# Two score banks masked apart, the first chunk's loads halved over two queues, fewer warm-up products, and a new order of the work

## The chip, the core and the metric

The kernel runs on one core of a Trainium2 chip. The metric is device time in microseconds (us) of one execution; an execution under the profiler also leaves a trace. The core has a matrix engine (TensorE: PE, with its weight loads as PEld), a vector engine (VectorE: DVE), a scalar engine (ScalarE: ACT), a general engine (GpSimd: POOL) and SyncE (SP), which issues most of the transfers. Each works through its own list of instructions in order; semaphores hold an instruction until what it needs is there.

## What is computed

Two batches of 768 positions, model width 512 (8 heads of 64). Three layers follow each other:

```python
# 1 retention: a decayed running state per head
state = gamma * state + k_t (outer) v_t ;  x_t = scale * q_t @ state
# 2 spectral layer
theta = x @ w_theta ;  zr, zi = x * cos(theta), x * sin(theta)
u = x + w_tok_r @ zr + w_tok_i @ zi          # over the 768 positions
x = u + relu(u @ w_ch)
# 3 gated layer
h = gelu(x @ w_in) ;  u, v = halves of h
v = (v - mean) / sqrt(var + 1e-6) * g_ln ;  v = w_sg @ v + b_sg
out = x + (u * v) @ w_out
```

## The kernel before

**Tiling.** Retention runs over 12 chunks of 128 positions (`i` = 0 to 11, six per batch). A chunk has, on PE, `scores` (8 products of 64x128 by 128x128, both operands float32), `outer` (8 products for the new state) and `attend` (8 products with the masked scores, and for all but a batch's first chunk 8 more with the state); on DVE, `mask` (the two score banks times a causal triangle, line 470), the state's `grow` (lines 512 and 519) and the copy of `x` out of PSUM (line 570); on ACT, `fade_v_heads` (line 488: eight small scalings of V); on POOL, `shrink` (line 522). The trace shows each float32 product of these as two records.

**The large products** are done three times over on split values: every operand is a high part in float32r (ACT, line 302) and a low remainder (DVE, line 308), and `terms3` multiplies high by high, low by high and high by low. They are 128x512 products: `angle` (six of them per half), `mix_main` (six), `mix_rest` (twelve of half width), then layers of twelve. A `turn` is four transposes on PE (line 664). The weights of these arrive packed and take two DVE operations at line 394 before they can be split.

**PSUM** has eight banks, which the kernel holds in one tile, `banks`; a planner gives every intermediate result a bank. The mask of a chunk reads both of its score banks with one operation, as a slice from the lower bank `a` to the higher bank `b` in steps of `b - a`:

```python
in0=banks.rearrange("p (b n t) -> p b n t", b=8, n=NP)[:, a : b + 1 : b - a]
```

**Loads.** `load_qk` and `load_kv` bring a chunk's Q and K, and its K and V, 512 KB each. They go through SP's queue, but for the first chunk's `kv`, which ACT issues (line 433). `dec` (the decay factors, line 453) is SP's second transfer, and the fade of every chunk reads it.

**Order.** `ORDER` is a table of operation numbers. `Plan.schedule` walks it with assumed durations, gives buffers and banks, and the operations are then issued by their assumed start. The order on an engine is thus set by that table. Ahead of everything PE does eight products on a zeroed tile; `keep_warm` puts products of the identity with itself in places where the planner expects PE to wait early on (before `WARM`, 34):

```python
gap = o.start - done
if done < WARM and gap > 0.25:
    keep_warm(idle[0], int(gap / 0.24))
```

Of the kernel before, what the change touches and what calls it, by code (L numbers as in the profile page):

```python
# [14 lines left out]
ALU = mybir.AluOpType  # L15
# [3 lines left out]
P = 128  # L19
NCH = S // P  # L20
# [42 lines left out]
class Plan:  # L63
# [3 lines left out]
    BEGIN = {"PE": 4.2, "ACT": 2.3, "DVE": 1.4, "POOL": 2.0, "SP": 0.8, "SPA": 0.8}  # L67
    FLY = 8

# [3 lines left out]
    def op(self, eng, dur, fn, r=(), w=(), prio=0.0, port=False, after=(), until=None, lev=None):  # L73
# [13 lines left out]
        o.lev = prio if lev is None else lev  # L87
        for x in r:
            self.res[x][1].append(o)
# [6 lines left out]

    def schedule(self, order):

# [6 lines left out]
        port = sent = skew = 0.0  # L105
        landed, last = [], {}
        for o in (self.ops[k] for k in order):
            t = max([engines[o.eng], *(d.end + (self.LAT if d.eng != o.eng else 0.0) for d in o.deps)])
# [4 lines left out]
            for b in o.bufs:  # L113
                if b.base is None:
                    room = free[b.of]
                    b.base = min(range(len(room)), key=lambda k: room[k])
                    if room[b.base]:
                        t = max(t, room[b.base] + self.LAT)
                    room[b.base] = math.inf
            o.start = t  # L120
            if o.eng in ("SP", "SPA"):
                engines[o.eng] = t + 0.45
                if sent < t + 1.0:
                    sent, skew = t + 1.4, 0.3
                sent += o.dur
                skew = min(2.8, skew + 0.25 * o.dur)
                o.end = sent + skew
                if o.eng == "SP":
                    landed.append(o.end)
            else:  # L130
                engines[o.eng] = o.end = t + o.dur
# [65 lines left out]
def retention_spectral_gmlp(  # L197
# [248 lines left out]
    def retention(i):  # L446
# [117 lines left out]
        if c > 0:  # L564
            r += [qk, ("state", c % 2)]
# [652 lines left out]
```

## Time and profile before

| | |
|---|---|
| median of 3 runs | 383.7 us (383.68 to 383.85) |
| profiled execution, its own time | 384.12 us |
| its span, first to last instruction | 382.4 us |
| PE busy | 374.5 us, 98% |
| DVE busy | 269.9 us, 71% |
| ACT busy | 173.6 us, 45% |
| chain that ended last | PE 97%, DMA 1%, DVE 1% |

The span is what the rows below measure; the execution's own time holds some 1.7 us more around it. Busy counts every record, identity products of `keep_warm` too, so a busy PE is not all useful work. Idle time of an engine that nobody waits for costs nothing.

### The profile page before, as it was taken

What the parts mean: (1) busy time and instruction counts of PE and PEld (TensorE: products, weight loads), DVE (VectorE), ACT (ScalarE), POOL (GpSimd) and SP (SyncE); (2) the same over time, 40 slices, a digit from 0 to 9 for tenths busy, and PEclk for the clock granted to TensorE, in tenths of its full rate; (3) what the DMA queues carried; (4) which work ended last, traced back from release to release, by engine and by line L of the source; (5) the groups of instructions that cost most, each with busy time, mean ns of one, the idle gap of its engine ahead of it and who ended that gap; (6) DMA issues with size and microseconds to landing.
All of it is one profiled execution on the core that took longest, in us unless ns stands there. A gap on an engine that the chain in (4) does not pass through costs nothing.

```text
span 382.4 us, 5777 instructions
## 1 busy us (share of the span) xinstructions
PE 374.5 (98%) x2404; PEld 317.2 (83%) x2404; DVE 269.9 (71%) x396; ACT 173.6 (45%) x292; POOL 15.1 (4%) x18
## 2 busy tenths in 40 slices
PE   8999999998999989999999999999999999999996
PEld 7878888886899868888899888888888888898885
DVE  1689899796887678586647548895996774628522
ACT  4577987633246524446322434755364662202000
POOL 1021040001200001000000000000000000000000
PEclk9999999999999999999999999999999999999999
DMA  8999018115326301630423001000000000000206
GB/s 311 413 409 416 23 33 315 68 41 219 111 111 257 129 0 35 241 132 36 153 96 110 2 27 27 2 28 0 3 0 0 3 0 0 2 0 2 82 2 248
DMA packets 10203, 39.06 MB, mean 102 GB/s; under 512 B 1216, under 2 KB 2240, under 8 KB 7744
## 3 DMA queue, kind: packets, MB, share of 16 engines
q1 hardware_dynamic: 10032, 38.15, 26.4%
q10 hardware_dynamic: 144, 0.52, 0.3%
q8 instruction: 19, 0.31, 0.3%
q14 instruction: 8, 0.07, 0.1%
HBM read 35.53 MB, written 3.15 MB: 101 GB/s over the span
## 4 chain that ended last, share of the span: by engine, by line
PE 97%; DMA 1%; DVE 1%; issue 0%
PE banks L282 95%; PE banks L664 2%; DMA b<-qkv 1%; DVE b L470 1%; DVE b L672 0%; DVE xb L570 0%; DVE b L1043 0%
## 5 line engine op out<-in xcount | busy, mean ns | idle before, releaser
L282 PE MATMUL banks<-b,b 128*128 128x512 f32 (+2 forms) x1788 | 332.9, 352 | 2.7 <-DVE b L470 2.7
L282 PEld LDWEIGHTS banks<-b,b 128*128 128x128 f32 (+1 forms) x1788 | 277.6, 183 | 50.7 <-issue 4.2
L302 ACT ACTIVATE b<-b 128x512 fp32r<-128x512 f32 (+1 forms) x61 | 50.6, 847 | 84.1 <-DVE b L394 31.6
L308 DVE TENSOR_TENSOR b<-b,b 128x512 fp32r<-128x512 f32 (+1 forms) x61 | 56.3, 939 | 12.5 <-ACT b L302 11.1
L394 DVE SCALAR_TENSOR_TENSOR b<-b 128x1024 int32<-128x1024 int32 x32 | 39.2, 1224 | 2.4 <-ACT b L374 1.9
L805 ACT ACTIVATE b<-banks 128x512 f32<-128x512 f32 x24 | 13.8, 590 | 31.0 <-PE banks L282 29.6
L470 DVE TENSOR_TENSOR b<-banks,causal 128x1024 f32<-128x1024 f32 x12 | 14.7, 1222 | 15.4 <-PE banks L282 15.3
L813 DVE SCALAR_TENSOR_TENSOR b<-b,banks 128x512 f32<-128x512 f32 x24 | 16.1, 684 | 13.4 <-ACT b L805 13.4
L302 ACT ACTIVATE b<-xa 128x512 fp32r<-128x512 f32 (+1 forms) x26 | 16.9, 666 | 18.8 <-DVE xa L793 7.8
L282 PEld LDWEIGHTS banks<-b 64*128 64x128 f32 (+1 forms) x352 | 17.9, 170 | 5.3 <-issue 2.7
L282 PE MATMUL banks<-b 64*128 64x128 f32 (+1 forms) x352 | 21.2, 264 | 0.5 <-DMA b<-qkv 0.5
L374 ACT ACTIVATE b<-b 128x1024 f32<-128x1024 f32 x16 | 18.1, 1138 | 5.3 <-DMA b<-wts 5.3
L823 ACT ACTIVATE b<-b 128x512 f32<-128x512 f32 x24 | 14.7, 627 | 10.6 <-DVE b L813 10.6
L308 DVE TENSOR_TENSOR b<-xa,b 128x512 fp32r<-128x512 f32 (+1 forms) x26 | 19.2, 742 | 0.4 <-ACT b L302 0.2
L829 DVE SCALAR_TENSOR_TENSOR b<-b,banks 128x512 f32<-128x512 f32 x24 | 16.2, 682 | 4.2 <-ACT b L823 2.4
L984 DVE SCALAR_TENSOR_TENSOR b<-banks,gcol,brow 128x512 f32<-128x512 f32 x12 | 8.7, 748 | 14.0 <-PE banks L282 14.0
L488 ACT ACTIVATE b<-b,dec 128x64 f32<-128x64 f32 x64 | 16.0, 337 | 3.9 <-DMA dec<-decays 3.9
L522 POOL TENSOR_TENSOR state<-grown,dec 128x256 f32<-128x256 f32 x8 | 11.7, 1458 | 113.8 <-DVE grown L519 96.9
L672 DVE TENSOR_TENSOR b<-banks,b 128x1024 f32<-128x1024 f32 x12 | 14.6, 1218 | 1.2 <-ACT b L647 1.1
L914 ACT ACTIVATE b<-b,rstd 128x512 f32<-128x512 f32 x12 | 9.3, 805 | 6.9 <-DVE rstd L903 6.9
L302 ACT ACTIVATE b<-xb 128x512 fp32r<-128x512 f32 (+1 forms) x13 | 8.6, 668 | 7.6 <-DVE xb L793 3.5
L383 DVE TENSOR_SCALAR b<-b 128x1024 int32<-128x1024 int32 x16 | 11.4, 713 | 0.8 <-DMA b<-wts 0.8
(58 smaller groups left out, 180.5 us busy)
## 6 DMA issues: line engine op xcount, KB each, us to landing
b<-wts SPq DMA_DIRECT2D x16, 1024.0 KB, 4.8
b<-qkv SPq DMA_DIRECT2D x23, 512.0 KB, 9.6
out<-b SPq DMA_DIRECT2D x11, 256.0 KB, 2.7
b<-wsg SPq DMA_DIRECT2D x9, 256.0 KB, 5.1
xa<-wts SPq DMA_DIRECT2D x2, 1024.0 KB, 10.8
xb<-wts SPq DMA_DIRECT2D x1, 1024.0 KB, 8.6
b<-qkv ACTq DMA_DIRECT2D x1, 512.0 KB, 4.9
brow<-bvec SPq DMA_DIRECT2D x1, 384.0 KB, 5.3
```

Source lines behind the costliest of these rows:

```text
L282: nc.tensor.matmul(out=o, lhsT=l, rhs=r, start=start, stop=stop)
L302: act(words, lambda: A.activation(out=hi(), in_=src(), func=AF.Copy), prio=prio, r=r, **k)
L308: lambda: E.tensor_tensor(out=lo(), in0=src(), in1=hi().bitcast(F32), op=ALU.subtract),
L374: lambda: A.activation(out=words(1).bitcast(F32), in_=words(1).bitcast(F32), func=AF.Copy, scale=REBIAS),
L394: lambda scalar=scalar, op=op: V.scalar_tensor_tensor(out=words(0), in0=words(1), scalar=scalar, in1=words(0), op0=op, op1=ALU.bitwise_or,),
L470: V.tensor_tensor(out=ap(at[i]).rearrange("p (h n t) -> p h n t", h=2, n=NP), in0=banks.rearrange("p (b n t) -> p b n t", b=8, n=NP)[:, a ...
L488: A.activation(out=v, in_=v, func=AF.Copy, scale=dk[:, h : h + 1])
L672: V.tensor_tensor(out=z2, in0=ap(tp)[:, None, :].to_broadcast([P, 2, 512]), in1=z2, op=ALU.mult)
L805: lambda: A.activation(out=ap(s), in_=ap(t), func=AF.Square),
L813: lambda: V.scalar_tensor_tensor(out=ap(s), in0=ap(s), scalar=1.0 / GA, in1=ap(t), op0=ALU.add, op1=ALU.mult),
L823: lambda: A.activation(out=ap(s), in_=ap(s), func=AF.Tanh, scale=GA * GC),
L829: lambda: V.scalar_tensor_tensor(out=ap(o), in0=ap(s), scalar=1.0, in1=ap(t), op0=ALU.add, op1=ALU.mult),
```

## The change

Four things change. `mask` becomes two operations of half the size, one for each score bank, and each names only its own bank. The first chunk's two loads become four: the upper 64 rows of each go by SP's queue, the lower 64 by ACT's. `keep_warm` acts only on expected waits over 0.8, and for 0.5 less of each. And the planner gets other assumed durations, separate lags between engines and costs for a change of product form, and `ORDER` is a new table, so that nearly all operations stand in another order; after the change there are four identity products in one place, where there were twenty in three.

```diff
@@ -64,13 +64,14 @@
 
 
     LAT = 0.15
-    BEGIN = {"PE": 4.2, "ACT": 2.3, "DVE": 1.4, "POOL": 2.0, "SP": 0.8, "SPA": 0.8}
+    BEGIN = {"PE": 4.9, "ACT": 2.3, "DVE": 1.4, "POOL": 2.0, "SP": 0.8, "SPA": 0.8}
     FLY = 8
+    OVER = {"ACT": 0.097, "DVE": 0.083, "POOL": 0.03}
 
     def __init__(self, room):
         self.ops, self.res, self.room = [], {}, room
 
-    def op(self, eng, dur, fn, r=(), w=(), prio=0.0, port=False, after=(), until=None, lev=None):
+    def op(self, eng, dur, fn, r=(), w=(), prio=0.0, port=False, after=(), until=None, lev=None, form="main"):
         deps, bufs = set(after), []
         for x in r:
             deps.update(self.res.setdefault(x, ([], []))[0])
...
+    def lag(self, a, b):
+        if a == "PE":
+            return 0.2 if b != "PE" else 0.0
+        if b == "PE":
+            return 0.1
+        return 0.06 if a in ("SP", "SPA") else 0.035 if b != "POOL" else 0.08
+
+    def switch(self, a, b):
+        tiled = ("scores", "outer", "attend")
+        if a in ("main", "turn") and b in tiled:
+            return 0.09 if a == "main" else 0.23
+        return {"attend": 0.09 * (b != "outer"), "outer": 0.07}.get(a, 0.0) * (a != b)
+
...
 ORDER = [
-    56, 57, 58, 84, 83, 0, 111, 110, 59, 60, 61, 87, 62, 64, 63, 85, 65, 137, 138, 66, 7, 75, 86,
...
+    56, 57, 58, 59, 60, 86, 87, 0, 115, 114, 61, 62, 64, 63, 88, 67, 91, 90, 65, 142, 68, 143, 89,
...
 ]
 
 
...
@@ -414,30 +436,22 @@
 
     load = {}
 
-    def load_qk(i):
+    def load_half(i, k):
         b, c = divmod(i, NCH)
-        load[i, 0] = Buf("pair")
-        dma(
-            512,
-            lambda: nc.sync.dma_start(out=ap(load[i, 0]), in_=qkv[b, c, 0]),
-            w=[load[i, 0]],
-            prio=early(i) - 12,
-            after=[gate[i - 3]] if i >= 3 else (),
-        )
-
-    def load_kv(i):
-        b, c = divmod(i, NCH)
-        load[i, 1] = Buf("pair")
-        dma(
-            512,
-            lambda: (nc.scalar if i == 0 else nc.sync).dma_start(
-                out=ap(load[i, 1]), in_=qkv[b, c, 1]
-            ),
-            eng="SPA" if i == 0 else "SP",
-            w=[load[i, 1]],
-            prio=early(i) - 11,
-            after=[gate[i - 3]] if i >= 3 else (),
-        )
+        x = load[i, k] = Buf("pair")
+
+        def rows(queue, a, e):
+            queue.dma_start(out=ap(x)[a:e], in_=qkv[b, c, k][a:e])
+
+        t = dict(prio=early(i) - 12 + k, after=[gate[i - 3]] if i >= 3 else ())
+        if i == 0:
+            dma(256, lambda: rows(nc.sync, 0, 64), w=[(x, "top")], **t)
+            dma(256, lambda: rows(nc.scalar, 64, P), eng="SPA", w=[(x, "low")], **t)
+        else:
+            dma(512, lambda: rows(nc.sync, 0, P), w=[(x, "top"), (x, "low")], **t)
+
+    def landed(x):
+        return [(x, "top"), (x, "low")]
 
     gate = {}
     xhl, at = {}, {}
@@ -446,8 +460,8 @@
     def retention(i):
         b, c = divmod(i, NCH)
         t = early(i)
-        load_qk(i)
-        load_kv(i)
+        load_half(i, 0)
+        load_half(i, 1)
         qk, kv = load[i, 0], load[i, 1]
         if i == 0:
             dma(264, lambda: nc.sync.dma_start(out=dec, in_=decays), w=["dk"], prio=t - 10.9)
@@ -455,26 +469,26 @@
 
         def scores():
             q, k = ap(qk)[:, 0:512], ap(qk)[:, 512:1024]
-            s = sorted(sc, key=lambda x: x.base)
             for p in range(NP):
                 for h in range(2):
                     rows = slice(h * D, (h + 1) * D)
                     cols = slice(p * P, (p + 1) * P)
-                    mm(ap(s[h])[:, cols], k[rows, cols], q[rows, cols], True, True)
-
-        pe(1.08, scores, r=[qk], w=sc, prio=t)
+                    mm(ap(sc[h])[:, cols], k[rows, cols], q[rows, cols], True, True)
+
+        pe(1.09, scores, form="scores", r=landed(qk), w=sc, prio=t)
         at[i] = Buf("pair")
 
-        def mask():
-            a, b = sorted(x.base for x in sc)
-            V.tensor_tensor(
-                out=ap(at[i]).rearrange("p (h n t) -> p h n t", h=2, n=NP),
-                in0=banks.rearrange("p (b n t) -> p b n t", b=8, n=NP)[:, a : b + 1 : b - a],
-                in1=causal[:, None, None, :].to_broadcast([P, 2, NP, P]),
-                op=ALU.mult,
-            )
-
-        dve(1024, mask, ps=True, r=sc, w=[at[i]], prio=t + 1)
+        for h in range(2):
+
+            def mask(h=h):
+                V.tensor_tensor(
+                    out=ap(at[i])[:, h * 512 : (h + 1) * 512].rearrange("p (n t) -> p n t", n=NP),
+                    in0=ap(sc[h]).rearrange("p (n t) -> p n t", n=NP),
+                    in1=causal[:, None, :].to_broadcast([P, NP, P]),
+                    op=ALU.mult,
+                )
+
+            dve(512, mask, ps=True, r=[sc[h]], w=[(at[i], h)], prio=t + 1)
 
         def fade_v():
             v3 = ap(kv)[:, 512:1024].rearrange("p (h d) -> p h d", h=H)
...
@@ -560,10 +574,10 @@
                         c == 0 or p == NP - 1,
                     )
 
-        r = [kv, (kv, 1), at[i]]
+        r = [*landed(kv), (kv, 1), (at[i], 0), (at[i], 1)]
         if c > 0:
-            r += [qk, ("state", c % 2)]
-        gate[i] = pe(0.98 if c == 0 else 2.0, attend, r=r, w=[xp], prio=t + 3)
+            r += [*landed(qk), ("state", c % 2)]
+        gate[i] = pe(0.93 if c == 0 else 1.95, attend, form="attend", r=r, w=[xp], prio=t + 3)
         keys = [("x", b, c, d) for d in range(NP)]
         dve(
             512,
...
@@ -1129,9 +1143,9 @@
     for o in plan.schedule(ORDER):
         if o.eng == "PE":
             gap = o.start - done
-            if done < WARM and gap > 0.25:
+            if done < WARM and gap > 0.8:
                 idle = [k for k in range(8) if used.get(k, 0.0) <= done and k not in [b.base for b in o.bufs]]
-                keep_warm(idle[0], int(gap / 0.24))
+                keep_warm(idle[0], int((gap - 0.5) / 0.24))
             done = o.end
         if o.eng == "ACT" and not loaded:
             nc.scalar.preload_act_table_set("silu_and_others")
```

PE's first rows before, from the eight products on the zeroed tile; `b_96` is chunk 0's qk (so `banks<-b_96` is its scores), `b_98` its kv, `b_118` its masked scores, `ident` the identity; `b_101` and `b_103` are chunk 1's kv and qk:

```order
L282 MATMUL banks<-state_82 128x128 x8
L282 MATMUL banks<-b_96 128x128 x8
L282 MATMUL banks<-ident 128x128 x14
L282 MATMUL banks<-b_98 64x64 x8
L282 MATMUL banks<-b_118,b_98 64x128 x8
L282 MATMUL banks<-b_103 128x128 x8
L664 MATMUL banks<-ident,xa_85 128x128 x4
L282 MATMUL banks<-b_101 64x64 x8
L282 MATMUL banks<-ident 128x128 x2
L282 MATMUL banks<-b_103,state_83 64x128 x8
L282 MATMUL banks<-b_188,b_101 64x128 x8
L282 MATMUL banks<-ident 128x128 x4
```

The same place after the change; `b_99` is now chunk 0's kv and `b_120` its masked scores, `b_103` and `b_105` are chunk 1's qk and kv:

```order
L304 MATMUL banks<-state_82 128x128 x8
L304 MATMUL banks<-b_96 128x128 x8
L304 MATMUL banks<-ident 128x128 x4
L304 MATMUL banks<-b_103 128x128 x8
L304 MATMUL banks<-b_120,b_99 64x128 x8
L304 MATMUL banks<-b_99 64x64 x8
L678 MATMUL banks<-ident,xa_85 128x128 x4
L304 MATMUL banks<-b_105 64x64 x8
L304 MATMUL banks<-b_103,state_83 64x128 x8
L304 MATMUL banks<-b_160,b_105 64x128 x8
```

Four identity products are left of fourteen, the two and the four further down are gone, and chunk 1's scores and chunk 0's attend now stand ahead of chunk 0's outer.

PE before, in batch 1, around the attend of chunk 10 (its two rows read `state_82` and `b_1235`); the 128x512 rows are parts of `mix_main`, the last row is chunk 10's outer:

```order
L282 MATMUL banks<-b_619,b_1239 128x512
L282 MATMUL banks<-b_640,b_1227 128x512
L282 MATMUL banks<-b_720,state_82 64x128 x8
L282 MATMUL banks<-b_1235,b_1175 64x128 x8
L282 MATMUL banks<-b_619,b_1227 128x512
L282 MATMUL banks<-b_619,b_1239 128x512
L282 MATMUL banks<-b_640,b_1227 128x512
L282 MATMUL banks<-b_619,b_1227 128x512
L282 MATMUL banks<-b_619,b_1239 128x512
L282 MATMUL banks<-b_640,b_1227 128x512
L664 MATMUL banks<-ident,xb 128x128 x4
L282 MATMUL banks<-b_1175 64x64 x8
```

PE after the change, where the same chunk's small products stand; `64x64` rows are outers of chunks 10 and 9, `128x128` rows the scores of chunks 9, 11 and 10, `64x128` rows the attends of chunks 9, 10 and 11, and the last row a turn:

```order
L304 MATMUL banks<-b_846 64x64 x8
L304 MATMUL banks<-b_728 64x64 x8
L304 MATMUL banks<-b_1155 128x128 x8
L304 MATMUL banks<-b_1152 128x128 x8
L304 MATMUL banks<-b_1170 128x128 x8
L304 MATMUL banks<-b_1155,state_83 64x128 x8
L304 MATMUL banks<-b_1254,b_728 64x128 x8
L304 MATMUL banks<-b_1170,state_82 64x128 x8
L304 MATMUL banks<-b_1285,b_846 64x128 x8
L304 MATMUL banks<-b_1152,state_83 64x128 x8
L304 MATMUL banks<-b_1267,b_837 64x128 x8
L678 MATMUL banks<-ident,xb 128x128 x4
```

The last three chunks' small products, which stood in separate places among the large ones, now follow each other in one run.

SP before and after, the first rows (`dec` is the decay factors, `xb<-wts` the first packed weight):

```order
L422 DMA b_96<-qkv 128x1024
L453 DMA dec<-decays 128x524
L433 DMA b_101<-qkv 128x1024
L422 DMA b_103<-qkv 128x1024
L363 DMA xb<-wts 128x2048
L433 DMA b_106<-qkv 128x1024
L422 DMA b_108<-qkv 128x1024
```

```order
L444 DMA b_96<-qkv 64x1024
L444 DMA b_99<-qkv 64x1024
L467 DMA dec<-decays 128x524
L444 DMA b_103<-qkv 128x1024
L444 DMA b_105<-qkv 128x1024
L385 DMA xb<-wts 128x2048
L444 DMA b_108<-qkv 128x1024
L444 DMA b_110<-qkv 128x1024
```

Chunk 0's kv has come to SP's queue as a half, and chunk 1's qk now stands ahead of its kv.

## Rows read from the trace of the kernel before

**Rows 1.** The page's first line: the span of the profiled execution.

```profile
span 382.4 us, 5777 instructions
```

**Rows 2.** Waits of PE: engine, line waited for, us in total, times, longest.

```profile
PE banks L282 <- DVE b L470: 2.7, 2, 1.4
PE banks L282 <- DMA b<-qkv: 0.5, 1, 0.5
```

**Rows 3.** Timeline of PE, start: start, us, operation, records, idle time before.

```profile
1.26 3.78 PE L282 MATMUL banks<-state 128*128 128x128 f32 x16 [1.26 <-DVE state L261]
5.51 1.91 PE L282 MATMUL banks<-b 64*128 64x128 f32 x16 [0.47 <-DMA b<-qkv]
7.35 3.39 PE L282 MATMUL banks<-ident 128*128 128x128 f32 x28
10.67 0.69 PE L282 MATMUL banks<-b 128*64 128x64 f32 x16
...
14.45 0.71 PE L282 MATMUL banks<-ident 128*128 128x128 f32 x4
...
17.14 1.16 PE L282 MATMUL banks<-ident 128*128 128x128 f32 x8
...
24.27 1.66 PE L282 MATMUL banks<-b,b 128*128 128x512 f32 x6
```

**Rows 4.** Timeline of ACT and DVE, start.

```profile
6.43 3.93 ACT L488 ACTIVATE b<-b,dec 128x64 f32<-128x64 f32 x16 [3.94 <-DMA dec<-decays]
...
7.54 1.23 DVE L470 TENSOR_TENSOR b<-banks,causal 128x1024 f32<-128x1024 f32 x1 [6.33 <-PE banks L282]
...
12.28 0.69 DVE L570 TENSOR_TENSOR xa<-banks,dec 128x512 f32<-128x512 f32 x1 [0.42 <-PE banks L282]
```

**Rows 5.** Two stretches of the start: engines busy, granted PE clock, DMA share, GB/s.

```profile
1.20:3.70 2.50, 2.44 (x11) 2.44 (x12) 0.01 (x1) 1.28 (x1) 0.59 (x3) 1.00 0.68 208
1.20:5.00 3.80, 3.73 (x16) 3.49 (x16) 0.01 (x1) 1.28 (x1) 0.59 (x3) 1.00 0.79 275
```

**Rows 6.** The chain that ended last, its first transfer: start, us, what.

```profile
0.79 4.68 DMA b<-qkv
```

**Rows 7.** Timelines of PE and DVE, 86 to 93 us.

```profile
86.73 1.16 PE L282 MATMUL banks<-b 64*128 64x128 f32 x16
87.83 1.66 PE L282 MATMUL banks<-b,b 128*128 128x512 f32 x6
90.89 1.62 PE L282 MATMUL banks<-b,b 128*128 128x512 f32 x6 [1.41 <-DVE b L470]
...
89.52 1.23 DVE L470 TENSOR_TENSOR b<-banks,causal 128x1024 f32<-128x1024 f32 x1 [1.30 <-PE banks L282]
```

**Rows 8.** Timeline of PE, 137 to 144 us.

```profile
141.07 1.66 PE L282 MATMUL banks<-b,b 128*128 128x512 f32 x6 [1.33 <-DVE b L470]
```

**Rows 9.** Timeline of PE where small and large products alternate, 26 to 34 us.

```profile
26.95 1.66 PE L282 MATMUL banks<-b,b 128*128 128x512 f32 x6
28.54 1.09 PE L282 MATMUL banks<-b,state 64*64 64x128 f32 x16
29.56 1.09 PE L282 MATMUL banks<-b,b 128*64 128x128 f32 x16
30.48 0.64 PE L282 MATMUL banks<-b 128*64 128x64 f32 x16
31.05 1.09 PE L282 MATMUL banks<-b,state 64*64 64x128 f32 x16
...
33.09 0.66 PE L664 MATMUL banks<-ident,xa 128*128 128x128 f32 x4
```

**Rows 10.** One stretch with large products alone on PE.

```profile
212.00:292.00 80.00, 80.00 (x355) 66.24 (x354) 63.42 (x128) 42.69 (x72) 0.00 (x0) 1.00 0.03 11
```

**Rows 11.** DVE's groups by form: busy us, mean ns of one, idle before.

```profile
L394 DVE SCALAR_TENSOR_TENSOR b<-b 128x1024 int32<-128x1024 int32 x32 | 39.2, 1224 | 2.4 <-ACT b L374 1.9
```

**Rows 12.** One stretch with the retention chunks of batch 0.

```profile
24.00:60.00 36.00, 36.00 (x340) 28.77 (x338) 33.46 (x40) 28.40 (x61) 6.85 (x3) 1.00 0.51 198
```

More of the change, by code (lines that the diff above doesn't have):

```diff
@@ L87, in op @@
         o.lev = prio if lev is None else lev
+        o.form = form
         for x in r:
@@ L104, in schedule @@
                 todo[b] = todo.get(b, 0) + 1
-        port = sent = skew = 0.0
+        port = sent = 0.0
+        behind, form = 0.45, None
         landed, last = [], {}
         for o in (self.ops[k] for k in order):
-            t = max([engines[o.eng], *(d.end + (self.LAT if d.eng != o.eng else 0.0) for d in o.deps)])
+            t = engines[o.eng]
+            if o.eng == "PE":
+                t += self.switch(form, o.form)
+                form = o.form
+            t = max([t, *(d.end + self.lag(d.eng, o.eng) for d in o.deps)])
             if o.port:
@@ L116, in schedule @@
                     b.base = min(range(len(room)), key=lambda k: room[k])
-                    if room[b.base]:
-                        t = max(t, room[b.base] + self.LAT)
+                    t = max(t, room[b.base] + 0.1)
                     room[b.base] = math.inf
-            o.start = t
+            o.start, o.end = t, t + o.dur
             if o.eng in ("SP", "SPA"):
                 engines[o.eng] = t + 0.45
-                if sent < t + 1.0:
-                    sent, skew = t + 1.4, 0.3
+                if sent < t + 1.25:
+                    sent = t + 1.75
+                    if t > 20:
+                        behind = 0.4
+                if sent + o.dur > 15 and sent < 20:
+                    behind = 1.7
                 sent += o.dur
-                skew = min(2.8, skew + 0.25 * o.dur)
-                o.end = sent + skew
+                o.end = sent + behind
                 if o.eng == "SP":
@@ L130, in schedule @@
             else:
-                engines[o.eng] = o.end = t + o.dur
+                engines[o.eng] = t + max(0.05, o.dur - self.OVER.get(o.eng, 0.0))
             if o.port:
@@ L287, in act @@
     def act(words, fn, ps=False, **k):
-        dur = 0.21 + words * 0.83e-3 if words < 1024 else 0.085 + words * 1.06e-3
+        dur = 0.205 + words * 0.83e-3 if words < 1024 else 0.085 + words * 1.03e-3
         return plan.op("ACT", dur - (0.04 if ps else 0.0), fn, **k)
@@ L295, in pool @@
     def pool(words, fn, **k):
-        return plan.op("POOL", 0.15 + words * 2.25e-3, fn, port=True, **k)
+        return plan.op("POOL", 0.07 + words * 2.35e-3, fn, port=True, **k)
     def dma(kb, fn, eng="SP", **k):
@@ L488, in fade_v_heads @@
                 A.activation(out=v, in_=v, func=AF.Copy, scale=dk[:, h : h + 1])
-        k = dict(r=[kv, "dk"], w=[(kv, 1)], prio=t + 1)
+        k = dict(r=[*landed(kv), "dk"], w=[(kv, 1)], prio=t + 1)
         if i < C["FA"]:
-            plan.op("ACT", 1.95, fade_v_heads, **k)
+            plan.op("ACT", 2.01, fade_v_heads, **k)
         else:
@@ L505, in outer @@
                         mm(ap(kp)[rows, p * D : (p + 1) * D], kk[:, cols], vv[:, cols], True, True)
-            pe(0.6, outer, r=[(kv, 1), kv], w=[kp], prio=t + 2)
+            pe(0.52, outer, form="outer", r=[(kv, 1), *landed(kv)], w=[kp], prio=t + 2)
             def grow():
@@ L612, in angle @@
                 )
-            pe(1.37, angle, r=[*xhl[i], *wp[W_THETA + half]], w=[th], prio=t + 0.01 * half, lev=t)
+            pe(1.36, angle, r=[*xhl[i], *wp[W_THETA + half]], w=[th], prio=t + 0.01 * half, lev=t)
         kk = Buf(dtype=I32)
@@ L666, in turn @@
                 )
-        pe(0.43, turn, r=keys, w=[tp], prio=t + 5.3)
+        pe(0.35, turn, form="turn", r=keys, w=[tp], prio=t + 5.3)
         def times():
@@ L708, in part @@
                 )
-            mains[b] = pe(1.37, part, r=[*zhl[i], *wp[W_MAIN + s]], w=[y[b, d]], prio=prio + d * 0.1)
+            mains[b] = pe(1.36, part, r=[*zhl[i], *wp[W_MAIN + s]], w=[y[b, d]], prio=prio + d * 0.1)
         if s == NCH - 1:
@@ L739, in mix_rest @@
             pe(
-                1.45,
+                1.435,
                 part,
@@ L974, in gate_tile @@
         reads += [x for s in ws for x in whl[s]]
-        pe(4.1 if g < B else 4.35, products, r=reads, w=[t], prio=prio)
+        pe(4.08 if g < B else 4.315, products, r=reads, w=[t], prio=prio)
         m = Buf()
@@ L1039, in finish @@
             reads = [a for f in range(NP) for a in ghl[g, f]]
-            pe(1.45, products, r=[*reads, *wp[W_OUT], *wp[W_OUT + 1]], w=[t], prio=prio + b)
+            pe(1.44, products, r=[*reads, *wp[W_OUT], *wp[W_OUT + 1]], w=[t], prio=prio + b)
             dve(
```

89 rows, old and new, of the table ORDER are left out of this document.

## Prediction

> **What bounds the kernel now.** I read the page first, then the waits of PE, then PE's timeline at the start and around each wait, and last what its products cost next to each other. The span is 382.4 us [rows 1]; the profiled execution's own time is 384.12 and the median 383.7, so the median lies 1.3 above the span. PE is busy nearly throughout, and all its idle time after the start is two waits for the mask, 2.7 us together, beside 0.5 for the first load [rows 2]. So time can come only from the start, from those two waits, and from work on PE that is busy without being useful. A plain large product takes 80.0 / 355 = 0.226 us, six of them 1.36 [rows 10]. From some 144 us on PE runs almost nothing else, back to back, and what any order does there is worth little.
>
> **The start.** In the rows the granted clock reads 1.00 from the first microsecond [rows 5], but the eight products ahead of everything (sixteen records) take 3.78 us, 0.47 each, and the identity products take (10.67 - 7.35) / 14 = 0.24 [rows 3]: by durations PE begins at the lower of its levels, 1.2 GHz, and has the upper, 2.4, by 7.35.
>
> *First load.* It lands at 0.79 + 4.68 = 5.47 [rows 6], PE starts at 5.51, and had been ready since 1.26 + 3.78 = 5.04 [rows 3]. Up to 5.0 us 275 x 3.8 = 1045 KB had moved, the two 524 KB loads of chunk 0 together; up to 3.7 it was 208 x 2.5 = 520 KB [rows 5]. Landing comes some 0.5 after the bytes. With both queues carrying qk first, its bytes are in by about 3.7 and it has landed by some 4.3: PE starts at about 5.05, worth 0.46, no more since PE is not ready sooner. If the halves gain nothing, 0. The Trainium skill (DMA: Bandwidth & Descriptors, Issuing engines are not separate DMA queues) says that transfers started by different engines run on the same 16 DMA engines and interleave, so a second queue adds no bandwidth. The rows on bytes agree, and the pair of loads together can't land sooner. Read as no gain for qk either, the rule would make the sum 374.7 in place of 374.2. `dec`, behind the same bytes as before, lands as before.
>
> *Identity products.* Twenty stand there, 14 + 2 + 4 [rows 3], by 0.24 some 4.8 us; with four left, 3.8 go. That counts only as far as PE has something to do instead. ACT's fade of chunk 0 starts at 6.43, held by `dec`, and eight scalings take about 2 (sixteen take 3.93) [rows 4]; the fade is done at 8.4. Mask 0 is done at 7.54 + 1.23 = 8.77 [rows 4]. Chunk 0's outer started at 10.67 [rows 3]: it stood 2 us behind identity products. Now the new order, with durations from PE's rows: scores 0 5.05 to 6.9 (1.84 as before, at the low clock), four identity products to 7.85, scores 1 (87.83 - 86.73 = 1.10 [rows 7]) to 8.95. Two half masks, by the 512-word operation 0.69 each [rows 4], are through at about 8.4. Attend 0 (eight of the sixteen products of an attend that takes 1.94 [rows 9], 1.0) to 9.95, outer 0 to 10.45. The turn needs x, which DVE copies from 10.0 to 10.75: **a new wait of 0.3**. Then turn 0.66, outer 1 0.57 [both rows 9] (ACT's second fade, its kv now behind qk 1, ends near 11.0), attend 1 2.04, scores 2 1.09, outer 2 0.6, scores 3 1.09 and attend 2 2.05 follow and end at about 18.9. In front of attend 2 DVE has chunk 1's second half mask, `grow`, two operations at line 394 of 1.22 [rows 11] and mask 2, and reaches its end at about 16.9, just in time. There the first angle starts, at 24.27 before [rows 3]; of the work ahead of it a turn and an outer, 1.2, have moved behind. So the start gains 24.27 - 1.2 - 18.9 = 4.2; I take **4.1**. Bounds: 5.2 with no wait at all; 1.5 if each of the four small stages waits 0.7 more for DVE.
>
> **The two waits for the mask.** Chunk 9's scores end at 87.83 on PE, DVE is free, yet mask 9 starts only at 89.52, as the next product group on PE ends, and the group after it then starts when the mask is through, at 90.89 [rows 7]. That is what a slice from bank `a` to bank `b` does when it counts as touching the banks between: it waits for, and holds up, an accumulation in a bank that it never reads. The second is the same picture [rows 8]. Single-bank masks end both: **2.7**. The split costs DVE some 0.1 per chunk, 12 x (2 x 0.69 - 1.23) = 1.8 at most, and DVE had 24.00 to 60.00 with 33.46 busy [rows 12], so 2.5 of cover in its fullest stage; on the path nothing. Without that cover it is the 1.8. Lower bound for the gain 1.4, if one of them comes back elsewhere.
>
> **Changes of product form.** Six large products take 1.36 among themselves, but 28.54 - 26.95 = 1.59 with small float32 products on both sides; an attend takes 33.09 - 31.05 = 2.04 before a turn and 30.48 - 28.54 = 1.94 before an outer [rows 9, 10]. So a round trip from large to small products and back costs 0.23 + 0.10 = 0.33. From the first angle on, the order before leaves the large products 17 times for scores, outers or attends, the new one 4 times, in long runs; turns alone break in 5 times before and 9 times after. 13 x 0.33 = 4.3 comes back, 4 x 0.17 = 0.7 goes (a turn-only trip, which no row isolates, lies between 0 and 0.33; I take the middle), and 0.4 goes inside the longer runs: **3.2** net. Bounds: 1.0 if the change of form costs half of this and turns cost the full price, 4.3 if turns cost nothing.
>
> **What is late next.** PE now comes to each operand some 4 us earlier at 24 and 9 us earlier from 150 on. I counted DVE and ACT queues, by the durations above, up to places where the large products need a result: the first `mix_main` (after angle 3) would start near 48, its split z ends near 46; `mix_main` of chunk 1, near 59, its weight's low part near 58; the run of attends 9 to 11 has its masks 1 us ahead. So the margins are 1 to 2 us, and I add **0.5** for small misses (bounds 0 and 5).
>
> Sum: 382.4 - 4.1 - 2.7 - 3.2 + 0.5 = 372.9 span; by the median, 383.7 - 9.5 = **374.2**.
>
> **Rivals.** *DVE becomes the bound* between 24 and 120: it is 93% busy in 24 to 60 [rows 12] and PE asks for its results earlier. Speaking against it: DVE's own chain at the start moves forward with PE, as it waited for PE there (6.33 us for scores 0 [rows 4]). If margins of 1 to 2 turn into waits of 1 to 2 in three places, 3.5 us: 377.5. *The order's cost of form does not come back*: the price sits in the kind of product rather than in its neighbours; then 3.2 is lost, 377.4. The equal-sized groups of 1.36 and 1.59 speak against it. *The mask was not the cause*: DVE started late for an ordinary reason and PE waits as before: 376.9. *Slower:* the upper clock comes late. With 16 identity products gone and PE idle for moments, PE could stay at the lower level through the start; every microsecond of full-speed work then costs another one. To lose the whole 9.5 it would have to stay there for 19 us beyond 7.35, that is beyond 26 us; only past that point is the kernel slower, by 0.5 us for each further microsecond; with a rise at 30 us it is 385.5. The Trainium skill (TensorE: Matmul & The Clock Gate, Part 1) speaks for it: the low clock is the default and activity lifts it, so less filler may lift it later. By that rule alone I'd allow a rise some microseconds later; the rows give PE no pause above 0.5 in the new order of the start, so I hold it unlikely.
>
> **How the numbers follow.** As forecast, within 372.8 to 376: 0.65. DVE as the bound or several small waits, 376 to 379: 0.18. Form cost not back, or masks still waiting, 376.5 to 377.5: 0.09. More than one of these, 379 to 383: 0.04. Late clock, or an order that stalls outright, at 383 or above: 0.04. The range 372.6 to 379.2 leaves out less than 2 in 10, and is cut at the bottom where all waits are zero and turns cost half. A difference of 0.2%, 0.8 us, is about what a measurement tells from no change. Faster 0.95, same 0.02, slower 0.03.
>
> **What would show it.** PE's first scores at about 5.05; the first angle near 19 and not near 24; no wait of PE for a mask; the group of small products of chunks 9 to 11 in one row of the timeline; PE's idle time below 1.5 in all. Wrong, if PE's waits name DVE or ACT for more than 2 us, if sixteen records of scores take 1.9 after 8 us (low clock), or if the large products' total does not shrink.

## The result, and the profile after

The changed kernel takes 375.2 us (median of 4 runs, 375.02 to 375.6) against 383.74 (383.68 to 383.85): a ratio of 0.9779, 95% interval 0.9762 to 0.9796. The forecast was 374.2, within 372.6 to 379.2. The profiled execution took 375.16. The medians differ by 8.5, the spans of the two profiles by 9.0, as the profiled execution before, 384.12, lay 0.4 above its median; the accounts below are of the spans.

The page's first line and PE's busy time after; the span was 382.4 [rows 1].

```profile
span 373.4 us, 5719 instructions
PE 366.1 (98%) x2372; PEld 314.1 (84%) x2372; DVE 267.6 (72%) x408; ACT 171.8 (46%) x292; POOL 11.0 (3%) x18
```

PE's waits after (engine, line waited for, us in total, times, longest), which answer to [rows 2]:

```profile
PE banks L304 <- DMA b<-qkv: 2.5, 3, 1.3
PE banks L304 <- DVE state L283: 1.3, 1, 1.3
PE banks L678 <- DVE xa L584: 0.4, 1, 0.4
```

No wait for a mask is left, the turn waits 0.4 (0.3 was foreseen), and loads now hold PE for 2.5, where it was 0.5. PE's timeline at the start after, against [rows 3]; a row of `b,b 128*64` is an attend and holds the products behind it too, where they read the same names:

```profile
5.40 1.83 PE L304 MATMUL banks<-b 64*128 64x128 f32 x16 [0.35 <-DMA b<-qkv]
...
9.62 1.16 PE L304 MATMUL banks<-b 64*128 64x128 f32 x16 [1.30 <-DMA b<-qkv]
...
12.62 0.65 PE L678 MATMUL banks<-ident,xa 128*128 128x128 f32 x4 [0.36 <-DVE xa L584]
...
18.59 1.16 PE L304 MATMUL banks<-b 64*128 64x128 f32 x16 [0.87 <-DMA b<-qkv]
...
20.70 4.04 PE L304 MATMUL banks<-b,b 128*64 128x128 f32 x28
```

Scores 0 start at 5.40, not 5.05; scores 1 find their load 1.30 late, scores 3 theirs 0.87. The row at 20.70 is the second half of an attend (1.02, as the first half takes from 28.54 to 29.56 in [rows 9]) with twelve products of the first angles behind it, so the first angle starts at 21.72, not near 18.9. ACT's first fade after, which was at 6.43 [rows 4], and SP's first issues:

```profile
8.43 2.02 ACT L502 ACTIVATE b<-b,dec 128x64 f32<-128x64 f32 x8 [5.14 <-DMA dec<-decays]
```

```profile
0.78 1.46 SPq L444 DMA_DIRECT2D b<-qkv  x2
2.29 0.59 SPq L467 DMA_DIRECT2D dec<-decays  x1
```

Two issues of 64 rows occupy SP for 1.46, and `dec` is issued at 2.29 and read 2.0 later than before. The second stretch of [rows 5], and a longer one (engines busy, granted clock, DMA share, GB/s):

```profile
1.20:5.00 3.80, 3.73 (x16) 3.49 (x16) 0.01 (x1) 1.28 (x1) 0.59 (x3) 1.00 0.80 196
1.20:6.50 5.30, 4.88 (x26) 4.59 (x28) 0.01 (x1) 1.28 (x1) 0.59 (x3) 1.00 0.86 202
```

Up to 5.0 the transfers moved 196 GB/s, where before it was 275, with the DMA engines as busy as before (0.80 and 0.79): the halves are not only issued slowly, they move slowly. Last, where chunks 9 to 11 stand after:

```profile
119.19 4.18 PE L304 MATMUL banks<-b 128*64 128x64 f32 x80
...
128.41 1.09 PE L304 MATMUL banks<-b,b 128*64 128x128 f32 x16
129.43 0.66 PE L678 MATMUL banks<-ident,xb 128*128 128x128 f32 x4
```

Ten microseconds of small products run without a pause.

**Where the 9.0 of the span came from.** The last operation, DVE's, starts at 370.31 (after) and 379.12 (before) on the chains that ended last:

```profile
370.31 0.42 DVE b L1057
```

```profile
379.12 0.42 DVE b L1043
```

From the first angle to it, the new order takes 370.31 - 21.72 = 348.6; the old one took 379.12 - 24.27 = 354.85 [rows 3], plus the 1.2 of a turn and an outer that moved into this part: 356.05. So the part after the first angle gave 7.5 (forecast 2.7 + 3.2 - 0.5 = 5.4) and the start 24.27 - 1.2 - 21.72 = 1.35 (forecast 4.1).

### The profile page after: what moved, and what is told of

Read it like the earlier page. It is cut to its first block, busy times and chain, and to the rows that moved or that the text cites. A ratio compares the mean times of both kernels' runs of the same rounds, so it can differ in the third digit from the quotient of the medians.

```text
span 373.4 us, 5719 instructions
## 1 busy us (share of the span) xinstructions
PE 366.1 (98%) x2372; PEld 314.1 (84%) x2372; DVE 267.6 (72%) x408; ACT 171.8 (46%) x292; POOL 11.0 (3%) x18
## 4 chain that ended last, share of the span: by engine, by line
PE 94%; DMA 5%; ACTq 0%; DVE 0%; issue 0%
PE banks L304 93%; DMA b<-qkv 5%; PE banks L678 1%; ACTq L444 0%; DVE b L1057 0%
## 5 line engine op out<-in xcount | busy, mean ns | idle before, releaser
L304 PE MATMUL banks<-b 64*128 64x128 f32 (+1 forms) x352 | 19.8, 261 | 2.5 <-DMA b<-qkv 2.5
L484 DVE TENSOR_TENSOR b<-banks,causal 128x512 f32<-128x512 f32 x24 | 15.6, 684 | 8.3 <-PE banks L304 8.3
L1020 DVE TENSOR_TENSOR b<-banks,xa 128x512 f32<-128x512 f32 x8 | 5.5, 689 | 13.0 <-PE banks L304 13.0
L634 ACT ACTIVATE b<-banks 128x512 int32<-128x512 f32 x12 | 7.1, 592 | 10.9 <-PE banks L304 10.9
```

The source lines that it names most:

```text
L304: nc.tensor.matmul(out=o, lhsT=l, rhs=r, start=start, stop=stop)
L484: V.tensor_tensor(out=ap(at[i])[:, h * 512 : (h + 1) * 512].rearrange("p (n t) -> p n t", n=NP), in0=ap(sc[h]).rearrange("p (n t) -> p n t ...
```

## The experiments

Two theories had to be told apart from their rivals: that the halved loads cost the start some 2 us, and that masks and changes of product form gave the rest. The time of the kernel before lay between 383.29 and 386.25 beside these runs, with medians of 383.45 to 384.0. The spread has a visible part: scores 0 take 1.16 in some profiles and 2.08 in others, that is, TensorE is at its upper level (2.4 GHz) by then or still at the lower one. Differences of a microsecond in the start are therefore read from rows rather than from totals. The changed kernel itself was not run again beside them.

**Chunk 0's loads whole again**, on the changed kernel: qk by SP's queue, kv by ACT's.

```diff
-            dma(256, lambda: rows(nc.sync, 0, 64), w=[(x, "top")], **t)
-            dma(256, lambda: rows(nc.scalar, 64, P), eng="SPA", w=[(x, "low")], **t)
+            dma(256, lambda: rows(nc.sync, 0, P) if k == 0 else None, w=[(x, "top")], **t)
+            dma(256, lambda: rows(nc.scalar, 0, P) if k == 1 else None, eng="SPA", w=[(x, "low")], **t)
```

> The changed kernel, with chunk 0's two loads whole again: qk by SP's queue, kv by ACT's, as before the change. Theory A (transfers of 64 rows move at about half the rate, 202 GB/s up to 6.5 us against 312 before, and push the decay factors and every load behind them back by 2 us): ACT's first fade starts near 6.4 in place of 8.43, PE's waits for loads fall from 2.5 us to under 1, the first angle starts near 19.5 in place of 21.7, time 373.0. Theory B (the delay comes from the new order of the loads behind, qk 1 ahead of kv 1, which this kernel keeps): within 0.4 of 375.2.

Measured: 372.83 (372.45 to 373.68), ratio to the kernel before 0.9715, interval 0.9681 to 0.9749. The interval lies below the changed kernel's, which begins at 0.9762, but that is from other rounds, so the rows have to carry it. PE's timeline:

```profile
5.64 1.16 PE L304 MATMUL banks<-b 64*128 64x128 f32 x16 [0.59 <-DMA b<-qkv]
...
7.82 1.16 PE L304 MATMUL banks<-b 64*128 64x128 f32 x16
...
16.87 1.09 PE L304 MATMUL banks<-b,state 64*64 64x128 f32 x16
18.91 3.03 PE L304 MATMUL banks<-b,b 128*128 128x512 f32 x12
```

ACT's first fade, and the two stretches of the start:

```profile
6.50 2.02 ACT L502 ACTIVATE b<-b,dec 128x64 f32<-128x64 f32 x8 [4.01 <-DMA dec<-decays]
```

```profile
1.20:5.00 3.80, 3.73 (x16) 3.49 (x16) 0.01 (x1) 1.28 (x1) 0.59 (x3) 1.00 0.77 267
1.20:6.50 5.30, 4.64 (x30) 4.35 (x32) 0.01 (x1) 1.28 (x1) 0.59 (x3) 1.00 0.85 308
```

Rate and fade are back, scores 1 wait for nothing, and the first angle starts at 18.91. That is the forecast's 18.9, but in part by luck: the forecast counted scores 0 at the lower level (1.84), and here they took 1.16. Slow issue alone isn't the reason for the changed kernel's rate: from 5.0 to 6.5, when the last half had been issued for over 2 us, it moved 218 GB/s, and this kernel 412. Nor is the clock the reason for the later first angle. The kernel `small_apart`, further down, has the changed kernel's loads and its start, and its profile has scores 0 at the upper level too:

```profile
5.62 1.16 PE L304 MATMUL banks<-b 64*128 64x128 f32 x16 [0.57 <-DMA b<-qkv]
...
20.86 4.06 PE L304 MATMUL banks<-b,b 128*64 128x128 f32 x28
```

Its first angle starts 1.02 into the last row, at 21.88, which is 3.0 later than with whole loads at the same level.

**Halves by columns**, on the changed kernel: the same two queues, but each half covers all 128 rows.

```diff
+        def columns(queue, a, e):
+            queue.dma_start(out=ap(x)[:, a:e], in_=qkv[b, c, k][:, a:e])
...
-            dma(256, lambda: rows(nc.sync, 0, 64), w=[(x, "top")], **t)
-            dma(256, lambda: rows(nc.scalar, 64, P), eng="SPA", w=[(x, "low")], **t)
+            dma(256, lambda: columns(nc.sync, 0, 512), w=[(x, "top")], **t)
+            dma(256, lambda: columns(nc.scalar, 512, 1024), eng="SPA", w=[(x, "low")], **t)
```

> The changed kernel, with chunk 0's loads still halved over the two queues, but by columns: each half fills all 128 rows. Theory A (it is the 64 rows that halve the rate): over 270 GB/s up to 5 us, PE's first scores at 5.05 to 5.2, time 372.7. Theory C (any halving costs, by more transfers to issue): rate and time as with halves by rows, 375.2, first scores at 5.4.

Measured: 373.21 (372.42 to 373.37). One stretch, then PE:

```profile
1.20:5.00 3.80, 3.73 (x18) 3.51 (x18) 0.01 (x1) 1.28 (x1) 0.59 (x3) 1.00 0.89 289
```

```profile
4.98 2.08 PE L304 MATMUL banks<-b 64*128 64x128 f32 x16
...
8.52 1.16 PE L304 MATMUL banks<-b 64*128 64x128 f32 x16 [0.29 <-DMA b<-qkv]
```

With halves of 128 rows the transfers move 289 GB/s, and scores 0 start when PE is ready, as the prediction had it (4.98, a little ahead of the expected 5.05). The first fade is at 7.23, since `dec` is still issued third on SP.

**Halves by rows, all four on SP's queue.**

```diff
-            dma(256, lambda: rows(nc.scalar, 64, P), eng="SPA", w=[(x, "low")], **t)
+            dma(256, lambda: rows(nc.sync, 64, P), eng="SPA", w=[(x, "low")], **t)
```

> The changed kernel, with all four halves by rows issued by SP, none by ACT. Theory A: each 64-row transfer runs at half the rate whatever its queue, so some 200 GB/s up to 6.5 us and a time of 375 to 377, first scores no earlier than 5.4. Theory D (the two queues hinder each other): the rate returns to about 300 GB/s and the time to about 373.

Measured: 375.52 in one run. Waits of PE, and a stretch:

```profile
PE banks L304 <- DMA b<-qkv: 2.9, 2, 2.1
```

```profile
1.20:6.50 5.30, 5.23 (x31) 4.79 (x32) 0.01 (x1) 0.86 (x1) 0.59 (x3) 1.00 0.78 193
```

One queue is as slow as two (193 and 202 GB/s), so it is not that queues disturb each other; it is the 64 rows. That scores 0 still started at 4.98 is a miss of theory A, which had said no earlier than 5.4; both qk halves now stood ahead of kv's instead of beside them, which would explain it. The price comes behind: `dec` is SP's fifth transfer, the first fade starts at 8.79, and scores 1 wait 2.1 for their load.

**Q and K by the two queues, kv whole on ACT's**, so that `dec` is SP's second transfer, beside a second set of the whole loads.

```diff
-            dma(256, lambda: rows(nc.sync, 0, 64), w=[(x, "top")], **t)
-            dma(256, lambda: rows(nc.scalar, 64, P), eng="SPA", w=[(x, "low")], **t)
+            dma(256, lambda: columns(nc.sync, 0, 512) if k == 0 else None, w=[(x, "top")], **t)
+            dma(256, lambda: columns(nc.scalar, 512 * (1 - k), 1024), eng="SPA", w=[(x, "low")], **t)
```

> After the change, with chunk 0's qk halved by columns (Q by SP's queue, K by ACT's) and its kv whole on ACT's queue, so that dec is SP's second transfer again. Theory (the 64-row halves cost the start, and dec goes late by what is issued ahead of it on SP): scores 0 at 5.0 to 5.1 as in the column halves, the first fade at 6.5 to 6.9 as with whole loads, no wait for a load of more than 0.4 in all; 372.0 to 372.8, 0 to 0.8 under whole loads. Rival (the first scores are not what the rest waits for, since chunk 0's fade and PE's clock set the start): the same 372.8 as whole loads within 0.4. Rival two (ACT's extra issue pushes the fade or kv back): 373.2 or more.

> The kernel of whole_loads once more beside the one with Q and K halved, for the same chip and rounds: 372.8 as before by every theory, within 0.6; scores 0 at 5.6, first fade at 6.5.

Measured: 372.43 (372.25 to 373.46), ratio 0.9702 (0.9679 to 0.9725); the whole loads 373.37 (372.48 to 374.79), 0.9731 (0.9705 to 0.9756). Both lie below the changed kernel's 375.02 to 375.6; between them nothing is settled. The rows say where the gain of the halving goes: scores 0 start at 4.98, but the fade, now held by kv, at 6.74, and scores 3 wait 0.99 for their load, where the expectation allowed 0.4 for all loads together.

```profile
6.74 2.02 ACT L505 ACTIVATE b<-b,dec 128x64 f32<-128x64 f32 x8 [3.75 <-DMA b<-qkv]
```

The profile of the second whole loads has scores 0 at 2.08 and the four identity products at 2.07, and its first angle at 20.95 instead of 18.91: these 2 us are the lower clock level, not the loads. So whole loads save 0.8 to 2.8 of the changed kernel's 21.72, by when the clock rises.

**The masks alone**, on the kernel before.

```diff
-            a, b = sorted(x.base for x in sc)
-            V.tensor_tensor(
-                out=ap(at[i]).rearrange("p (h n t) -> p h n t", h=2, n=NP),
-                in0=banks.rearrange("p (b n t) -> p b n t", b=8, n=NP)[:, a : b + 1 : b - a],
...
+            for h, s in enumerate(sorted(sc, key=lambda x: x.base)):
+                V.tensor_tensor(
+                    out=ap(at[i])[:, h * 512 : (h + 1) * 512].rearrange("p (n t) -> p n t", n=NP),
+                    in0=ap(s).rearrange("p (n t) -> p n t", n=NP),
...
```

> The kernel before, with one edit: each mask is two operations in place of one, one for each score bank. If the slice over the banks between was the cause of PE's two waits for the mask, both are gone (2.7 us) and the time is 381.0. If the mask started late for another reason, the waits stay and the time is 383.7 or some tenths more, by the longer masks.

Measured: 380.27 (379.84 to 382.07, 10 runs), ratio 0.9904 (0.9877 to 0.9931). All of PE's waits:

```profile
PE banks L282 <- DVE state L261: 1.3, 1, 1.3
PE banks L282 <- DMA b<-qkv: 0.5, 1, 0.5
```

Both mask waits are gone. Its first angle and its last DVE operation:

```profile
25.30 1.66 PE L282 MATMUL banks<-b,b 128*128 128x512 f32 x6
```

```profile
376.77 0.42 DVE b L1043
```

They are 351.47 apart, against 354.85 before: 3.4, more than the 2.7 of idle time. Half of the rest is in [rows 7]: six products that start at 87.83 would let the next start at 89.19 (1.36 later), and it started at 90.89, so the wait cost 1.70 where the view counts 1.41 of idleness. The 0.3 is the time in which the last products end without a successor beside them (their row takes 1.66, not 1.36). The other wait stands behind an attend, whose row runs only 0.07 past the start of what follows, and its share of the excess was not taken apart. DVE's busy time rose by 1.3 (269.9 to 271.2), and no wait of PE names it.

**The old mask in the new order.** One operation over both banks, in place of the later of the two.

```diff
+                seen.append(h)
+                if len(seen) == 1:
+                    return
+                lo, hi = sorted(x.base for x in sc)
...
-                    in0=ap(sc[h]).rearrange("p (n t) -> p n t", n=NP),
+                    in0=banks.rearrange("p (b n t) -> p b n t", b=8, n=NP)[:, lo : hi + 1 : hi - lo],
```

> The changed kernel with the mask as one operation on the slice over both score banks again, in the place of the later of the two. If the slice holds up what lies in the banks between, the new order suffers at least as much as the old one: PE waits for the mask return, 2.7 us or more in all, time 378 or more. If the single-bank masks gave nothing by themselves: 375.2 within 0.4.

Measured: 385.72 in one run, span 383.9, 10.5 above the changed kernel's. Its main wait, and PE where the longest stands:

```profile
PE banks L304 <- DVE b L490: 6.7, 5, 2.5
```

```profile
134.16 1.79 PE L304 MATMUL banks<-b,state 64*64 64x128 f32 x16 [2.55 <-DVE b L490]
135.88 1.97 PE L304 MATMUL banks<-b,b 128*64 128x128 f32 x16
137.78 1.09 PE L304 MATMUL banks<-b,state 64*64 64x128 f32 x16
```

DVE's masks of the next chunks, just ahead of that wait:

```profile
131.65 2.36 DVE L490 TENSOR_TENSOR b<-banks,causal 128x1024 f32<-128x1024 f32 x2 [3.30 <-PE banks L304]
```

The granted clock from 134.1 to 140.0:

```profile
134.10:140.00 5.90, 5.84 (x66) 4.87 (x67) 4.11 (x7) 3.85 (x6) 0.61 (x1) 0.71 0.01 3
```

The new order needs masks that name one bank: where it lays small products of several chunks in one run, masks that reach over the banks between start only when another chunk's attend has ended (131.65), and the attend behind them only when both masks have (134.16). Of the 10.5, idle time is 6.7, and 1.6 is the clock: after 2.55 of pause the two halves of the attend take 1.72 and 1.90 instead of 1.02 each, and the granted clock of that stretch is 0.71. The other 2.2 were not taken apart; only one of the five waits stands behind large products, where 0.3 would come on top.

**No identity products: before, and after the change.** In each, `keep_warm` makes none.

```diff
-        for _ in range(n):
+        for _ in range(0):
```

> The kernel before, without its twenty identity products. Theory of the prediction: PE stood up to 2 us behind them at chunk 0's outer and 1 to 1.7 further down, so 2 to 3 us come back: 381.2. Rival (they only fill waits that are there anyway): 383.7. Rival (they keep the clock up): PE's scores after 8 us take 1.9 in place of 1.1 and the time is 385 or more.

> The changed kernel without its last four identity products: PE then idles from about 7.2 to 9.6 us, when chunk 1's qk lands. If they are hidden behind that wait and the clock does not need them: 375.2 within 0.3, scores 1 still 1.1. If the clock falls in the pause: scores 1 takes up to 1.9 and the time is 376 to 378.

Before without its twenty: 380.73 (380.1 to 380.98), ratio 0.9904 (0.9866 to 0.9942). PE:

```profile
6.91 1.94 PE L282 MATMUL banks<-b 128*64 128x64 f32 x15 [0.18 <-ACT b L488]
...
20.29 1.66 PE L282 MATMUL banks<-b,b 128*128 128x512 f32 x6
```

The first angle comes 4.0 earlier (24.27 [rows 3]), of which 0.75 is the clock (scores 0 in 1.16, not 1.91); the filler did stand in the way, and ACT, which follows head by head, is ready for the outer at 6.91. In the changed kernel without its four, 376.21 in one run, the other side shows. PE, then a stretch, and the same stretch of the changed kernel:

```profile
5.31 1.16 PE L304 MATMUL banks<-b 64*128 64x128 f32 x16 [0.31 <-DMA b<-qkv]
9.49 2.08 PE L304 MATMUL banks<-b 64*128 64x128 f32 x16 [3.02 <-DMA b<-qkv]
```

```profile
9.00:14.00 5.00, 4.51 (x46) 4.29 (x48) 1.15 (x2) 3.31 (x14) 0.00 (x0) 0.50 1.02 414
```

```profile
9.00:14.00 5.00, 4.03 (x72) 3.53 (x74) 2.81 (x5) 4.56 (x17) 0.00 (x0) 1.00 1.03 419
```

PE had been at the upper level (1.16 for scores 0), stood still for 3.02 behind the late load, and ran at 0.50, which is the 1.2 GHz level, from 9 to 14 us: the span is 1.1 longer. This is the lower level of the forecast's slower rival, come back in a kernel that gives it a pause. The Trainium skill (TensorE: Matmul & The Clock Gate, Part 1) has the clock depend on how busy TensorE has lately been, and this run agrees with it: 0.50 after 3.02 of rest, 1.00 in the changed kernel, whose identity products leave 1.30.

**What a change of product form costs.** 96 extra products of the identity's upper 64 rows, 64x128 by 64x128 in float32, which nobody reads: in one run ahead of the first group of large products of the layers, or four ahead of each of 24 groups.

```diff
+            if 142 <= nth < 166:
+                free = [k for k in range(8) if used.get(k, 0.0) <= o.start and k not in [b.base for b in o.bufs]]
+                small(free[0], 96 if nth == 142 else 0)
+            nth += 1
```

The other kernel has `small(free[0], 4)` there.

> The changed kernel with 96 extra float32 products of the identity's upper half with itself (64x128 by 64x128) in one run ahead of the first layer group, near 185 us, into an idle bank. They are extra work: some 0.13 us each, 12 to 14 us, so 388. It is the other arrangement's yardstick.

> The same 96 extra float32 products, four ahead of each of 24 layer groups in place of 96 at one place: 23 more round trips from large to small products and back. If a round trip costs 0.2 to 0.33 us by itself, 4.6 to 7.6 us more than with all 96 together. If the price sits in the products and not in their neighbours: the same time within 0.5.

Measured: 398.05 together and 406.82 apart, one run each. The last long row of the chain that ended last (start, us, instructions) holds all of them; first the changed kernel's, then together, then apart:

```profile
143.70 226.59 PE banks L304 x1146
```

```profile
144.74 248.42 PE banks L304 x1338
```

```profile
143.87 258.08 PE banks L304 x1338
```

The same 1338 records take 9.66 longer with 23 more changes of form there and back: 0.42 each, above the expected 0.2 to 0.33. The 96 products in one run cost (248.42 - 226.59) / 96 = 0.23 each, not the 0.13 that the expectation took from products that come in pairs of row groups; that miss is in both and leaves the difference alone.

## Why the prediction was right, point by point

- **The masks (2.7): right, and mis-sized.** The waits came from banks that the mask did not read; naming one bank ends them, in the old order too. The term is 3.4: behind large products a wait cost 0.3 beside its idle time, and 0.4 of the excess stays open.
- **The changes of form (3.2): right, and mis-sized.** By subtraction they are 7.5 - 3.4 = 4.1, with whatever small misses there are in it. The price of a round trip was read as 0.33 from neighbours in [rows 9, 10] and measured at 0.42, but with products that all sit in the upper 64 rows, which the kernel's own do not; that the kernel's trips cost 0.42 is not shown. At that price 13 trips would give 5.5, at the forecast's price 4.3. What was priced too high is the turn. Rows after the change, twelve large products and one turn in the first pair, two turns in the second:

```profile
69.03 3.00 PE L304 MATMUL banks<-b,b 128*128 128x512 f32 x12
...
72.21 4.15 PE L304 MATMUL banks<-b,b 128*128 128x512 f32 x17
```

```profile
129.84 3.00 PE L304 MATMUL banks<-b,b 128*128 128x512 f32 x12
...
133.48 1.85 PE L304 MATMUL banks<-b,b 128*128 128x512 f32 x7
```

The first pair is 3.18 apart, the second 3.64: a second turn adds 0.46, and one by itself takes 3.18 - 2 x 1.36 = 0.46 as well. So leaving the large products for a turn costs nothing that these rows show, where 0.17 was assumed, and the forecast's own bound of 4.3, for turns that cost nothing, came nearer than its 3.2.

- **Small misses (0.5):** none. After 18.6 PE waits for nothing, though the margins were counted as 1 to 2 us.
- **The start (4.1): the one step that failed in its reason.** "With both queues carrying qk first ... it has landed by some 4.3" and "`dec`, behind the same bytes as before, lands as before" did not hold. PE began at 5.40, `dec` let the fade begin 2.0 later, and loads held scores 1 and scores 3 for 1.30 and 0.87. The start gave 1.35, below the bound of 1.5 that the forecast had set for it, with the 16 identity products saved but 2.2 of new waits for loads. Whole loads put the first angle at 18.91 or 20.95, by when the clock rises. I weighed what a second queue does, and not what a transfer of 64 rows does. The Trainium skill (DMA: Bandwidth & Descriptors, Rules for kernel authors) advises against two transfers to separate halves of the partitions: they share the engines either way. The runs agree and go further: 196 GB/s against 267 with whole loads in the same stretch.
- **The sum came close because two errors cancel:** 2.75 too much for the start, 2.1 too little for the rest (0.7 masks, 0.9 form, 0.5 misses). The remaining 0.2 lies behind the last DVE operation.
- **The rivals.** DVE as the bound: no wait of PE names it after 12.62. The form's cost not coming back: a trip does cost (0.42 in the experiment), and by subtraction 4.1 came back. Masks not the cause: the masks alone gave 3.4. The late clock: not in the changed kernel's profile, but the profile of the small products together, whose start is the same, still has scores 1 at the lower level (2.08 at 9.89) and its first angle at 22.78, 1.06 later; and 3.02 of pause bring that level back.

## What to carry to other kernels

Halving the first loads paid nothing that these runs can tell: by rows it slowed them, and by columns it brought the first scores forward by 0.6 but pushed `dec` or another load back. Before splitting what stands first in a queue, look at what stands second, and keep all 128 rows in each part. In this kernel a slice that steps over other banks waited for them as well, so name each bank by itself, above all before an order is packed more tightly. Where small float32 products alternate with large ones, count the changes of form and gather the small ones, and price a PE wait behind large products as its idle time and some 0.3 more.

## What the runs showed of the hardware that was not expected

- Loads that cover 64 of 128 rows move slowly on one queue or two: 196 and 181 GB/s from 1.2 to 5.0 us, 267 to 289 for the same data in 128 rows; from 5.0 to 6.5 it is 218 and 221, against 412 with whole loads. The issue of one took SP 0.6 to 0.8 (two in 1.46, four in 2.48), against 0.38 for the first whole load.
- TensorE's rise to the upper level at the start differs between executions of one kernel by enough to move the first angle by 2 us (18.91 and 20.95 with the same whole loads). Pauses of 2.55 and 3.02 were followed by stretches at a granted clock of 0.71 and 0.50, one of 1.30 in the changed kernel and one of 2.06 with all halves on SP's queue by 1.00 from 9 to 14 us.
